# Two tiles of attention output turned by DMA instead of TensorE, in a linear-attention plus GEGLU kernel

## The chip, the cores and the metric

The kernel runs on one core of one Trainium2 chip. The metric is the device time of one execution in microseconds (us); lower is better. A core has five engines with an instruction queue each, which work in order and wait for one another through semaphores: TensorE (PE), VectorE (DVE), ScalarE (ACT), GpSimd (POOL) and SyncE (SP). SP and POOL here mostly issue DMAs, which 16 DMA engines carry out.

## The reference

Eight batches, eight heads, 576 positions, head width 64. The result of the attention is laid out as 4608 tokens by 512 channels and goes through a gated feed-forward layer of width 1536. What is computed, cut to what matters:

```python
def phi(x, c, s):                       # c, s: cos and sin of the position
    r = np.maximum(x, 0.0)
    return np.concatenate([r * c, r * s], axis=-1)      # 64 -> 128 features
q_p, k_p = phi(q, cos_w, sin_w), phi(k, cos_w, sin_w)
kv  = np.einsum('bhsf,bhsd->bhfd', k_p, v)
z   = np.sum(k_p, axis=2)
num = np.einsum('bhsf,bhfd->bhsd', q_p, kv)
den = np.einsum('bhsf,bhf->bhs', q_p, z)[..., None] + 1e-06
x   = (num / den) as 4608 x 512
g   = x @ w_gate
out = (gelu(g) * (x @ w_val)) @ w_out
```

## The kernel before, in words

**Attention, by batch.** `prep` (L151) makes one column group of `phi(q)` or `phi(k)`: the cosine half on DVE (L161) or the sine half on ACT (L159); `js` are the nine column groups of a batch. `kv_unit` multiplies keys and values of a batch. `turn_q` (L190) transposes `phi(q)` of a batch with two DMA transposes on SP's queue, as `turn_j` does on TensorE for the first two batches. `nm_unit` (L279) takes one tile of 128 positions: eight matmuls (L281), then three DVE instructions (`den`, `rec` and the product `x_sb`, L292 to L294). A batch has five such tiles; tile 4 overlaps tile 3 by half.

**Turning a tile.** The feed-forward layer wants x with the channels on the partitions. `turn_x_pe` (L352) does this with four TensorE transposes into PSUM (L356) and an ACT copy for each piece (L360); `turn_x` (L345) does it with one DMA transpose for each piece on SP's queue (L348). A piece is the part of a tile that lies in one block of 512 tokens. Tile 3 of batch 1 has two pieces: 64 tokens at the end of block 1, and 64 at the start of block 2.

**Feed-forward, by block.** Nine blocks `n` of 512 tokens, twelve units `jt` of 128 hidden columns. `gv_unit` (L366) does one unit: four gate matmuls into one PSUM bank, four value matmuls into the next (L375), Gelu on ACT (`gel`, L383), the product with the value bank on DVE (`hT`, L384). It uses two pairs of banks in turn, so unit u+2 needs the banks of unit u again: its gate matmuls wait for the Gelu of unit u, and its value matmuls for the product of unit u. A unit can be done for half of the tokens only (`c0`, `w`), which makes matmuls of 256 columns instead of 512. `o_part` (L402) multiplies by `w_out` for one tile of 128 tokens (L405), copies the result on ACT (L414) into one of four `o_sb` buffers, and puts it on the list `stores`; `flush` (L397) issues what is on the list, two DMAs of 128 KB for each tile.

**The order of the work** is written out by hand: each engine runs its instructions in the order in which the program issues them. Around the change it is as follows. The list `order` (L528) runs the output parts of block 0 between the turns and tiles of batch 1, and ends with the turn of tile 2. Then comes block 1 in the loop at L584. Its first two units are in halves, in the order (unit 0, low), (unit 1, low), (unit 0, high), (unit 1, high), with tile 3 turned behind the first of them. The low half of block 1 is made of tile 4 of batch 0, tile 0 and half of tile 1 of batch 1; the high half of tiles 1, 2 and 3. Between the units stand the last column groups of `phi(q)` of batch 2, then `turn_q(2)`, tile 4 of batch 1, and `phi(k)` of batch 2 in thirds (`prep_third`). The table `q3` says behind which unit each column group of `phi(q)` of batch 3 is made. The q of batch 3 is loaded by SP ahead of block 1 (L556). POOL's queue carries loads, and at the end the two casts of v of batch 2 (L558).

Of the kernel before, what the change touches and what calls it, by code (L numbers as in the profile page):

```python
# [16 lines left out]
def kernel(  # L17
# [13 lines left out]
    nc = tc.nc  # L31
# [8 lines left out]
    R = S // 64  # L40
# [4 lines left out]
    JA = 4  # L45
# [31 lines left out]
    def load(eng, name, b, m0, m1, j0=0, j1=R):  # L77
        if (name, b) not in staged:
            staged[name, b] = inp.tile([128, NP, R * D], FP32, name=name + "f")
        eng.dma_start(  # L80
            out=staged[name, b][:, m0:m1, j0 * D:j1 * D],
            in_=rows(srcs[name], b)[:, m0:m1, j0 * D:j1 * D],
        )
# [67 lines left out]
    def prep(name, b, part, js, m0=0, m1=NP, eng=None):  # L151
        dst = phi_tile(name, b)
        src = staged[name, b]
        tab = (cos_t, sin_t)[part]
        for j in js:
            o = dst[:, m0:m1, j, part * D:(part + 1) * D]
            i = src[:, m0:m1, j * D:(j + 1) * D]
            if eng is nc.scalar:
                nc.scalar.activation(o, i, AF.Relu, scale=tab[:, j:j + 1])  # L159
            else:  # L160
                (eng or nc.vector).tensor_scalar(  # L161
                    o, i, 0.0, tab[:, j:j + 1], op0=ALU.max, op1=ALU.mult
                )
# [13 lines left out]
    def cast_v(b, m0, m1, copy, j0=0, j1=R):  # L177
        copy(  # L178
            vx_tiles[b % 2][:, m0:m1, j0:j1, 0:D],
            staged["v", b][:, m0:m1, j0 * D:j1 * D].rearrange("p m (j d) -> p m j d", d=D),  # L180
        )
# [8 lines left out]
    def turn_q(b):  # L190
        for i in range(2):
            nc.sync.dma_start_transpose(
                out=qt_tile(b)[:, i].rearrange("f m (j p) -> f (m j) p", p=64),
                in_=phi["q", b][64 * i:64 * i + 64].rearrange("p m j f -> p (m j f)"),
            )
# [156 lines left out]
    def turn_x_pe(b, t, to, copy):  # L352
        x = xs.pop((b, t))
        p = bank16(to)[:, 0:CT * 128].rearrange("p (c n) -> p c n", c=CT)
        for ct in range(CT):
            nc.tensor.transpose(  # L356
                out=p[:, ct, :], in_=x[:, ct * 128:(ct + 1) * 128], identity=ident
            )
        for blk, c, o, m in pieces(b, t):
            copy(xT_block(blk)[:, :, c:c + m], p[:, :, o:o + m])  # L360
# [5 lines left out]
    def gv_unit(n, jt, c0=0, w=BLK):  # L366
        xt = xT[n]
        js = slice(jt * 128, (jt + 1) * 128)
        b0 = 2 * (turn[0] % 2)
        turn[0] += 1  # L370
        if n not in hT:
            hT[n] = ffn.tile([128, JT, BLK], BF16, name="hT")
        for g, wt in ((0, wg_sb), (1, wv_sb)):
            for ct in range(CT):
                nc.tensor.matmul(  # L375
                    bank(b0 + g)[:, 0:w],
                    lhsT=wt[:, ct, js],
                    rhs=xt[:, ct, c0:c0 + w],
                    start=(ct == 0),
                    stop=(ct == CT - 1),  # L380
                )
        gel = ffn.tile([128, BLK], FP32, name="gel")
        nc.scalar.activation(gel[:, 0:w], bank(b0)[:, 0:w], AF.Gelu)  # L383
        nc.vector.tensor_mul(  # L384
            hT[n][:, jt, c0:c0 + w], gel[:, 0:w], bank(b0 + 1)[:, 0:w]
        )
# [3 lines left out]
    def store(engs, i, o_sb, c0=0, c1=C):  # L390

        for n, eng in enumerate(engs):
            b, j = divmod(2 * i + n, R)
            dst = out[b * S:(b + 1) * S, c0:c1].rearrange("(p j) c -> j p c", j=R)[j]
            eng.dma_start(out=dst, in_=o_sb[64 * n:64 * n + 64, c0:c1])

    def flush():  # L397
        for i, o_sb in stores:
            store((nc.sync, nc.sync), i, o_sb)
        stores.clear()  # L400

    def o_part(i, jts, to, copy):  # L402
        n, tt = divmod(i, 4)
        for jt in jts:
            nc.tensor.matmul(  # L405
                bank(to),
                lhsT=hT[n][:, jt, tt * 128:(tt + 1) * 128],
                rhs=wo_sb[:, jt, :],
                start=(jt == 0),
                stop=(jt == JT - 1),  # L410
            )
        if JT - 1 in jts:
            o_sb = outp.tile([128, C], FP32, name="o_sb")
            copy(o_sb, bank(to))  # L414
            flush()
            stores.append((i, o_sb))


# [1 line left out]
    HALF = BLK // 2  # L420
# [93 lines left out]
    for jt in range(JH, JT):  # L514
# [16 lines left out]
        + [("q8", 2), ("o", 1, 4), ("o", 2, 4), ("kv",), ("q2", 0, 2), ("o", 3, 4)]  # L531
        + [("nm", 0, 2), ("o", 0, 8), ("nm", 1, 6), ("o", 1, 8), ("xt", 0, 4), ("nm", 2, 2)]
        + [("q2", 2, 3), ("o", 2, 8), ("xt", 1, 5), ("nm", 3, 6), ("q2", 3, 4), ("o", 3, 8)]
        + [("xt", 2, 4)]
    )
    for what, *a in order:
        if what == "o":
# [15 lines left out]
            nm_unit(1, a[0], a[1])  # L553
        if what == "xt":
            turn_x_pe(1, a[0], a[1], act_copy)
    for m in (0, 2):  # L556
        load(nc.sync, "q", 3, m, m + 2)
    for m in (0, 2):  # L558
        cast_v(2, m, m + 2, pool_copy)


    def prep_third(name, b, i):
# [4 lines left out]
    def loads(b, names=("q", "k", "v")):  # L567
# [5 lines left out]


    q3 = {
        (1, 8): ((0,), (0, 1)),
        (1, 9): ((1,), (2, 3)),
        (1, 10): ((2,), (4, 5)),
        (1, 11): ((3, 4, 5), (6, 7)),
        (2, 0): ((6, 7), (8,)),  # L580
        (2, 1): ((8,), ()),
    }
    turn[0] = 1
    for n in range(1, NB):  # L584
        b = n + 1
        t_kv, t_nm, t_q, t_k = {1: (5, 8, 12, 12), 2: (5, 7, 7, 9), 3: (2, 5, 6, 9)}.get(
            n, (1, 2, 4, 8)
        )
        for jt in range(JT):
            if n > 3 or jt > 1:  # L590
                gv_unit(n, jt)
            else:
                for i in range(2):
                    gv_unit(n, i, jt * HALF, HALF)
                    if n == 1:
                        j = JA + 2 * jt + i
                        prep("q", b, 1, (j,), eng=nc.scalar)
                        prep("q", b, 0, (j,))
                        if jt == i == 0:
                            turn_x_pe(1, 3, 5, act_copy)  # L600
            if jt % 3 == 1:
                flush()
            if b < B:
                if n == 1 and jt == 2:
                    prep("q", b, 0, (R - 1,))
                    prep("q", b, 1, (R - 1,), eng=nc.scalar)
                    turn_q(b)
                    nm_unit(1, NT - 1)
                if n == 1 and jt == 3:
                    turn_x(1, NT - 1)  # L610

                late = -(-(BLK - 64 * b) // 128)
                nms = [(b, jt - t_nm)] if 0 <= jt - t_nm < (late if n == 1 else NT) else []
                if n == 2 and jt < 2:
                    nms.append((n, 3 + jt))
                i = jt - t_nm - 1
                if 0 <= i < late:
                    turn_x(b, i)
                    if n == 1 and i == late - 1:
                        loads(b + 1, ("k", "v"))  # L620
                for bt in nms:
                    nm_unit(*bt)
                if jt == t_kv:
                    kv_unit(b)
                i = jt - 2 if n <= 2 else -1
                if 0 <= i < 3:
                    prep_third("k", b, i)
                i = jt - (3 if n == 2 else 0)
                if n in (2, 3) and 0 <= i < 2:
                    cast_v(b, 2 * i, 2 * i + 2, dve_copy)  # L630
                i = jt - 9
                if n > 2 and 0 <= i < 2 and b + 1 < B:
                    cast_v(b + 1, 2 * i, 2 * i + 2, dve_copy)
                if (n, jt) in q3:
                    cosines, sines_ = q3[n, jt]
                    prep("q", 3, 1, sines_, eng=nc.scalar)
                    prep("q", 3, 0, cosines)
                if n > 1 and b + 1 < B:
                    if 0 <= jt - t_q < 3:
                        prep_third("q", b + 1, jt - t_q)  # L640
                    if 0 <= jt - t_k < 3:
                        prep_third("k", b + 1, jt - t_k)
                for c, t in nms:
                    if t == NT - 1:
                        if c + 1 < B:
                            turn_q(c + 1)
                        if c + 2 < B:
                            loads(c + 2)
                        for i in range(-(-(BLK - 64 * c) // 128), NT):
                            turn_x(c, i)  # L650
            if n > 1:
                o_part(
                    4 * (n - 1) + jt // 3,
                    range(4 * (jt % 3), 4 * (jt % 3) + 4),
                    4,
                    act_copy,
                )
# [47 lines left out]
```

## Time and profile before

| | |
|---|---|
| median of 5 runs | 329.09 us (327.19 to 329.83) |
| the profiled execution: its own time, its span | 327.04 us, 324.9 us |
| PE busy | 315.3 us, 97% of the span |
| DVE, ACT, POOL busy | 52%, 49%, 9% |
| mean granted TensorE clock | 0.998 |
| mean DMA rate | 165 GB/s |

The profile is of one execution; its time lies 2.05 us below the median of the runs, and its span 2.1 us below its own time. Times inside the trace count from the start of the span. A matmul's duration in the trace is modelled and overlaps the next one, so the spacing of TensorE work is read from starts.

### The profile page before, as it was taken

The page shows a single profiled execution, that of the slowest core. Times are in us where ns is not written, and L with a number is a line of the kernel's source. Part 1 is how long each engine was busy: PE and PEld are TensorE (multiplying, and loading weights), DVE is VectorE, ACT ScalarE, POOL GpSimd, SP SyncE. Part 2 cuts the span into 40 slices and gives each one's busy share as a digit, 9 for nine tenths or more (in the row PEclk, how much of TensorE's full clock was granted, in tenths as well). Part 3 has the DMA queues.
Part 4 walks back from the last instruction along what each step waited for, and adds up shares of the span by engine and source line. Part 5 has one row for each costly group of instructions (what it writes and reads, how often), then busy time and mean ns, then how long its engine had stood idle before and what let it go on. Part 6 is the DMA issues. An engine that isn't in the chain of part 4 may idle for free.

```text
span 324.9 us, 6295 instructions
## 1 busy us (share of the span) xinstructions
PE 315.3 (97%) x2401; PEld 164.9 (51%) x2438; DVE 167.8 (52%) x406; ACT 159.9 (49%) x341; POOL 28.3 (9%) x43
## 2 busy tenths in 40 slices
PE   8899999999999999999999999999999999999995
PEld 3585556556554564445544545445544444444443
DVE  5863666749665961793585348544532222222211
ACT  8865767947455833674457336642222333222220
POOL 2855462000000000000000000000000000000000
PEclk9999999999999999999999999999999999999999
DMA  7999999992999999989979992764531111111124
GB/s 264 259 190 273 303 347 335 221 137 50 307 135 356 241 99 255 296 161 173 366 154 128 305 292 46 105 105 99 90 70 35 35 32 32 35 32 32 34 66 97
DMA packets 69102, 53.57 MB, mean 165 GB/s; under 512 B 45392, under 2 KB 54352, under 8 KB 69072
## 3 DMA queue, kind: packets, MB, share of 16 engines
q1 hardware_dynamic: 59264, 41.23, 55.0%
q0 software_dynamic: 9648, 11.80, 15.8%
q8 instruction: 19, 0.31, 0.4%
q10 hardware_dynamic: 160, 0.13, 0.1%
q14 instruction: 11, 0.09, 0.1%
HBM read 37.75 MB, written 9.44 MB: 145 GB/s over the span
## 4 chain that ended last, share of the span: by engine, by line
PE 93%; DMA 3%; DVE 1%; issue 1%; SPq 1%; DVEq 0%
PE ps L375 57%; PE ps L405 27%; PE ps L281 3%; DMA qf<-in_q_dram 3%; PE ps L240 3%; PE ps L666 1%; SPq L80 1%; PE ps L203 1%; PE ps L356 1%; DVE qp L161 0%; DVE x_sb L321 0%; DVE hT L384 0%; DVE o_sb L673 0%; DVE rec L317 0%; PE ps L139 0%
## 5 line engine op out<-in xcount | busy, mean ns | idle before, releaser
L384 DVE TENSOR_TENSOR hT<-gel,ps 128x512 bf16<-128x512 f32 (+2 forms) x120 | 75.9, 634 | 131.8 <-PE ps L375 127.5
L383 ACT ACTIVATE gel<-ps 128x512 f32<-128x512 f32 (+2 forms) x120 | 66.7, 556 | 109.8 <-PE ps L375 106.1
L375 PE MATMUL ps<-xT,wg_sb 128*128 128x512 bf16 (+2 forms) x473 | 112.2, 357 | 0.6 <-issue 0.2
L375 PE MATMUL ps<-xT,wv_sb 128*128 128x512 bf16 (+2 forms) x472 | 112.2, 357 | 0.5
L405 PE MATMUL ps<-wo_sb,hT 128*128 128x512 bf16 x400 | 102.5, 379 | 1.6 <-issue 1.0
L375 PEld LDWEIGHTS <-wv_sb 128*128 128x128 bf16 x480 | 46.4, 98 | 47.4 <-DMA wv_sb<-in_moe_w_val_dram 0.4
L375 PEld LDWEIGHTS <-wg_sb 128*128 128x128 bf16 x480 | 45.8, 98 | 45.8
L405 PEld LDWEIGHTS <-hT 128*128 128x128 bf16 x420 | 38.4, 98 | 39.8
L414 ACT COPY o_sb<-ps 128x512 f32<-128x512 f32 x34 | 19.9, 585 | 29.4 <-PE ps L405 28.3
L159 ACT ACTIVATE qp<-qf,sin_t 128x256 bf16<-128x256 f32 x71 | 31.8, 502 | 1.7 <-DMA qf<-in_q_dram 1.7
L159 ACT ACTIVATE kp<-kf,sin_t 128x256 bf16<-128x256 f32 (+1 forms) x75 | 30.4, 477 | 0.9 <-DMA kf<-in_k_dram 0.9
L294 DVE TENSOR_TENSOR x_sb<-ps,rec 128x512 bf16<-128x512 f32 x38 | 26.3, 691 | 1.5 <-DVE rec L293 0.2
L161 DVE TENSOR_SCALAR qp<-qf,cos_t 128x256 bf16<-128x256 f32 x71 | 21.7, 353 | 4.3 <-DMA qf<-in_q_dram 4.3
L281 PEld LDWEIGHTS <-qT 128*128 128x128 bf16 x304 | 14.6, 98 | 7.7 <-issue 0.2
L161 DVE TENSOR_SCALAR kp<-kf,cos_t 128x256 bf16<-128x256 f32 x63 | 18.2, 348 | 0.0
L281 PE MATMUL ps<-kv_sb,qT 128*128 128x65 bf16 x304 | 16.0, 194 | 0.0
L249 ACT CAST kv_sb<-ps 128x260 bf16<-128x260 f32 x14 | 4.6, 382 | 13.1 <-PE ps L240 13.1
L139 PE MATMUL ps<-dummy 128*128 128x512 bf16 x28 | 9.0, 477 | 1.5 <-POOL dummy L113 1.5
L240 PEld LDWEIGHTS <-kp 64*128 64x128 bf16 x504 | 8.6, 94 | 3.1 <-issue 3.0
L178 DVE CAST vx<-vf 128x1152 bf16<-128x1152 f32 x12 | 9.2, 769 | 0.8 <-DMA vf<-in_v_dram 0.8
L240 PE MATMUL ps<-vx,kp 64*128 64x65 bf16 x504 | 9.5, 191 | 0.0
L293 DVE RECIPROCAL rec<-den 128x8 f32<-128x8 f32 x38 | 7.7, 203 | 1.3
(52 smaller groups left out, 91.6 us busy)
## 6 DMA issues: line engine op xcount, KB each, us to landing
out_dram<-o_sb SPq DMA_DIRECT2D x70, 128.0 KB, 2.5
kf<-in_k_dram SPq DMA_DIRECT2D x12, 576.0 KB, 6.6
vf<-in_v_dram SPq DMA_DIRECT2D x12, 576.0 KB, 8.8
qf<-in_q_dram SPq DMA_DIRECT2D x10, 576.0 KB, 5.4
qf<-in_q_dram POOLq DMA_DIRECT2D x4, 576.0 KB, 12.1
kf<-in_k_dram POOLq DMA_DIRECT2D x4, 576.0 KB, 12.8
vf<-in_v_dram POOLq DMA_DIRECT2D x4, 576.0 KB, 10.8
wg_sb<-in_moe_w_gate_dram POOLq DMA_DIRECT2D x6, 256.0 KB, 9.0
```

Of the source, the lines that this page charges most:

```text
L139: nc.tensor.matmul(bank(to), lhsT=dummy[:, 0:128], rhs=dummy, start=True, stop=True)
L159: nc.scalar.activation(o, i, AF.Relu, scale=tab[:, j:j + 1])
L161: (eng or nc.vector).tensor_scalar(o, i, 0.0, tab[:, j:j + 1], op0=ALU.max, op1=ALU.mult)
L178: copy(vx_tiles[b % 2][:, m0:m1, j0:j1, 0:D], staged["v", b][:, m0:m1, j0 * D:j1 * D].rearrange("p m (j d) -> p m j d", d=D),)
L240: nc.tensor.matmul(bank(6 + i)[:, m * (D + 1):(m + 1) * (D + 1)], lhsT=kp[rr, m, j, :], rhs=vx[rr, m, j, :], start=(j == 0), stop=(j == R ...
L281: nc.tensor.matmul(bank(b0 + h // 4)[:, (h % 4) * (D + 1):(h % 4 + 1) * (D + 1)], lhsT=q_cols(b, t, h), rhs=kv_sb[b][:, h // 2, h % 2, :], ...
L294: nc.vector.tensor_tensor(x, nm[:, :, :, 0:D], rec[:, :, :, None].to_broadcast([128, 2, 4, D]), op=ALU.mult,)
L375: nc.tensor.matmul(bank(b0 + g)[:, 0:w], lhsT=wt[:, ct, js], rhs=xt[:, ct, c0:c0 + w], start=(ct == 0), stop=(ct == CT - 1),)
L383: nc.scalar.activation(gel[:, 0:w], bank(b0)[:, 0:w], AF.Gelu)
L384: nc.vector.tensor_mul(hT[n][:, jt, c0:c0 + w], gel[:, 0:w], bank(b0 + 1)[:, 0:w])
L405: nc.tensor.matmul(bank(to), lhsT=hT[n][:, jt, tt * 128:(tt + 1) * 128], rhs=wo_sb[:, jt, :], start=(jt == 0), stop=(jt == JT - 1),)
L414: copy(o_sb, bank(to))
```

## The change

- Tiles 2 and 3 of batch 1 are turned by DMA on SP's queue (three DMA transposes) instead of on TensorE.
- In block 1 the first four units are in halves instead of the first two: four low halves, then four high halves. Column groups 4, 5, 6 and (7, 8) of `phi(q)` of batch 2 stand behind the four low halves.
- `turn_q(2)` comes behind unit step 1 instead of step 2.
- The load of q of batch 3 comes behind `turn_q(2)` on SP's queue, and its column groups start one unit later.
- The eight stores of block 0 are no longer issued by SP as the tiles come; GpSimd issues them all, behind its casts of v of batch 2.

```diff
-    def flush():
+    def flush(eng=nc.sync):
         for i, o_sb in stores:
-            store((nc.sync, nc.sync), i, o_sb)
+            store((eng, eng), i, o_sb)
         stores.clear()
...
             copy(o_sb, bank(to))
-            flush()
+            if n > 0:
+                flush()
             stores.append((i, o_sb))
...
-        + [("xt", 2, 4)]
     )
...
-    for m in (0, 2):
-        load(nc.sync, "q", 3, m, m + 2)
+    for t in (2, 3):
+        turn_x(1, t)
     for m in (0, 2):
         cast_v(2, m, m + 2, pool_copy)
+    flush(nc.gpsimd)
...
     q3 = {
-        (1, 8): ((0,), (0, 1)),
-        (1, 9): ((1,), (2, 3)),
-        (1, 10): ((2,), (4, 5)),
-        (1, 11): ((3, 4, 5), (6, 7)),
-        (2, 0): ((6, 7), (8,)),
-        (2, 1): ((8,), ()),
+        (1, 9): ((0,), (0, 1)),
+        (1, 10): ((1,), (2, 3)),
+        (1, 11): ((2, 3, 4), (4, 5, 6)),
+        (2, 0): ((5, 6), (7,)),
+        (2, 1): ((7, 8), (8,)),
     }
...
-            if n > 3 or jt > 1:
+            heads = (0, 4, 2, 2)[n] if n < 4 else 0
+            if jt >= heads:
                 gv_unit(n, jt)
             else:
                 for i in range(2):
-                    gv_unit(n, i, jt * HALF, HALF)
-                    if n == 1:
-                        j = JA + 2 * jt + i
-                        prep("q", b, 1, (j,), eng=nc.scalar)
-                        prep("q", b, 0, (j,))
-                        if jt == i == 0:
-                            turn_x_pe(1, 3, 5, act_copy)
+                    half, unit = divmod(2 * jt + i, heads)
+                    gv_unit(n, unit, half * HALF, HALF)
+                    if n == 1 and jt < 2:
+                        js = ((4,), (5,), (6,), (7, 8))[2 * jt + i]
+                        prep("q", b, 1, js, eng=nc.scalar)
+                        prep("q", b, 0, js)
...
+                if n == 1 and jt == 1:
+                    turn_q(b)
+                    loads(b + 1, ("q",))
                 if n == 1 and jt == 2:
-                    prep("q", b, 0, (R - 1,))
-                    prep("q", b, 1, (R - 1,), eng=nc.scalar)
-                    turn_q(b)
                     nm_unit(1, NT - 1)
```

## The prediction

> **What bounds the kernel now.** I read the chain that ended last first, then the busy times by stage, then the timeline where the change lies.
>
> ```profile
> PE 93%; DMA 3%; DVE 1%; issue 1%; SPq 1%; DVEq 0%
> ```
> ```profile
> 55.00:63.00 8.00, 7.95 (x66) 5.48 (x65) 5.60 (x15) 7.48 (x21) 2.04 (x2) 1.00 0.90 265
> ```
>
> The first line is the chain: 93% of the span is TensorE itself. The second is the stretch of the change, 55 to 63 us: TensorE is busy 7.95 of 8.00 us, DVE 5.60, ACT 7.48 (fifth and sixth pair of columns). So an edit here gains only what it takes from TensorE's stream, and loses whatever makes that stream wait. The next view is the timeline of that stretch.
>
> ```profile
> 53.53 0.69 DVE L294 TENSOR_TENSOR x_sb<-ps,rec 128x512 bf16<-128x512 f32 x1
> ...
> 54.88 0.69 DVE L294 TENSOR_TENSOR x_sb<-ps,rec 128x512 bf16<-128x512 f32 x1
> ...
> 56.20 0.39 PE L356 MATMUL ps<-ident,x_sb 128*128 128x128 bf16 x4
> ...
> 56.42 0.60 PE L375 MATMUL ps<-xT,wg_sb 128*128 128x256 bf16 x4
> ...
> 57.42 0.60 PE L375 MATMUL ps<-xT,wg_sb 128*128 128x256 bf16 x4
> ...
> 59.17 1.03 PE L375 MATMUL ps<-xT,wg_sb 128*128 128x512 bf16 x4
> ...
> 62.46 0.69 DVE L294 TENSOR_TENSOR x_sb<-ps,rec 128x512 bf16<-128x512 f32 x1
> ...
> 62.88 1.03 PE L375 MATMUL ps<-xT,wg_sb 128*128 128x512 bf16 x4
> 63.07 0.87 DVE L161 TENSOR_SCALAR kp<-kf,cos_t 128x256 bf16<-128x256 f32 x3
> ...
> 63.85 0.68 DVE L384 TENSOR_TENSOR hT<-gel,ps 128x512 bf16<-128x512 f32 x1
> ```
>
> The x of tile 2 is ready at 54.22 (53.53 + 0.69), of tile 3 at 55.57. The four transposes of a tile take 0.22 us of TensorE (56.20 to 56.42), a half unit 0.87 us (two from 57.42 to 59.17), a whole unit 1.73 us. Between 56.42 and 57.42 lies one half unit and 0.13 us of waiting for tile 3's copies. The last three DVE rows, from 62.46 on, belong to a burst in front of a product, which matters below. The last view is that of the line which turns tiles by DMA, over the whole span and from 70 to 83 us.
>
> ```profile
> L348 SPq DMA_TRANSPOSE xT<-x_sb x34: 1171/1242/2872, 70.7 to 236.3; - x34
> ...
> DMA to landing us min/median/max: 2.3/3.3/10.8
> ```
> ```profile
> DMA to landing us min/median/max: 2.4/2.4/2.9
> ```
>
> SP is taken 1.2 us by each issue, and the tile lands 2.3 to 2.5 us after its issue begins when the DMA engines are quiet, later behind other transfers (5.5 at 134.5, 9 to 10.8 behind six loads).
>
> **What the Trainium skill says.** VectorE: DVE Perf Modes, section The three transpose paths, gives 1309 ns for a DMA transpose of 128x128 and 390 ns for TensorE's. Here TensorE's cost 54 ns each in the stream (0.22 / 4), and a DMA issue 1.2 us, with 2.4 to land. DMA: Bandwidth & Descriptors, section Anatomy of one DMA, fits about 2.0 us plus bytes / 436e3; for a tile's 128 KB that is 2.3 us, as the trace has it, and says that latency, not volume, is the price. The same page, section Queues, rings and completion order, has each DMA engine take turns between queues packet by packet: GpSimd's stores will share with SP's transposes, not stand in front of them. No row of the trace shows the two together. TensorE: Matmul & The Clock Gate, section Architectural detail, calls ACT and DVE strictly first in, first out; the burst above agrees: the product at 63.85 could have started by 63.15 (its matmuls end at 62.88, and L384 follows by 0.27) and stood behind three cosines.
>
> **The change, part by part.**
>
> *Transposes off TensorE.* Eight go: 2 x 0.22 = 0.44 us from the path, and with the copies the wait of 0.13 us. Three copies go from ACT (0.62 + 2 x 0.35, 1.3 us), which is off the path.
>
> *Halves.* Two more whole units become four halves: 4 x 0.865 against 2 x 1.73 us, nothing on TensorE. The order after, by starts: low halves at 55.13 (tile 1's copy ends at 55.06), 56.00, 56.86, 57.73; high halves 58.60, 59.46; tile 4's `nm_unit` 60.33; high halves 60.58, 61.45; unit 4 at 62.31, against 62.88 before. **Gain 0.57 us**, if nobody is late.
>
> *The wait added.* The high half at 58.60 waits for the first two DMA transposes. SP is free now, the six stores ahead of it being gone: tile 2 issued 54.27 to 55.5, tile 3's first piece at 55.63, landing at 58.0 with 2.4 us. Slack 0.6 us. Who else is on the DMA engines: from 52 to 54.3 they are 98% busy with v(2) and the stores. From 52 to 56.2 v's queue moves 0.84 MB and SP's 0.42 MB; without SP's part, v needs 0.84 MB / 0.355 MB per us = 2.4 us and is done by about 54.4. GpSimd's casts (2 x 1.15) then end near 55.6, and its stores (0.72 us an issue, by its load rows) meet tile 3's landing. I put that at 0 to 0.6 us, which the slack holds: price 0. From both sides: 0, and 2.5 us if it takes 5.5 us as at 134.5. Behind this wait, TensorE's whole queue is held.
>
> *DVE's burst.* Halved units leave half the time between a product and the reuse of its bank. Behind the low halves DVE ends cosines 7 and 8 at about 59.9, the first two high products by 61.0; then the burst, tile 4's three instructions and three cosines of k(2), takes 1.91 us (before: 62.03 to 63.94). The product of the third high half comes at 62.85 to 63.27; unit 4's value matmuls want its bank at 62.31 + 0.87 = 63.18, and 0.07 for the semaphore. **Loss 0.15 us**; bounds 0 and 1.0, the latter if the sines of k(2) on ACT (1.30 us) also hold up the Gelu of that half, which my count ends 0.1 us before its bank is wanted. Before, the same product had 0.9 us to spare (64.53 against 65.46).
>
> *SP's queue.* It loses eight stores, gains three transposes. `turn_q(2)` goes from 62.26 to about 60.0, when the last sine and cosine of q(2) are done; its second half lands 2.2 us earlier than 73.0, where tile 0 of batch 2 wanted it at 73.07 without waiting. Price 0. The loads of q(3) move from 56.73 to about 68.5, behind that turn, and land after 4.7 and 5.5 us (those behind the next turn, at 96.15): 74.0. First use is on ACT behind unit 9's Gelu, near 74.4 (74.88 less the 0.4 gained). A lateness of 1 to 2 us there delays the next Gelu, not TensorE, two units ahead in banks: price 0; bounds 0 and 0.5. The turn of tile 4 follows the loads on SP, at 69.6 instead of 70.66. Behind three times the bytes the trace has 10.1 us; a third of the excess gives 5 us, so 74.6, wanted by block 2 near 78.6.
>
> *q(3)'s sines and cosines* bunch at units 11 and block 2's start: three sines before block 2's first Gelu instead of two, 0.45 us, while the product there waits for DVE in either case (80.75). `turn_q(3)` comes some 0.3 us later, wanted 3 us after its landing. Price 0.
>
> *Stores on POOL.* Nothing is queued behind them but the end. The four `o_sb` buffers are wanted again at 88.03; eight issues from 55.6 end near 61.4 and land by 65. Price 0.
>
> **Sum:** -0.57 + 0.15 = -0.42 us against the profiled 327.04, so 326.6; from unit 5 on TensorE's order is the same and gapless, so it is carried to the end. The profiled execution lies 2.05 us below the median; with the same offset the median goes from 329.09 to **328.7**. 0.5% is 1.6 us, about what a measurement of this kernel can tell from no change.
>
> **Rivals.**
> 1. *The tiles land late* (slower): TensorE waits at the first high half. For: 2.3 to 2.5 us needs quiet engines, and GpSimd's eight stores, never seen beside a transpose here, start just then. Against: v(2) is done by then, and they share. It decides from a landing of 3.4 us on (0.6 slack plus 0.42 gained); with 5.5 us it costs 2.5, so +2.1: 331.2. Chance 0.20, of which beyond +1.6 us less than half.
> 2. *ACT and DVE become the bound of the halved units*: the burst costs 1.0 instead of 0.15, +0.4: 329.5. For: ACT is 94% busy there. Against: three copies are taken from it. Chance 0.13.
> 3. *q(3) or tile 4 late*: the latter lands after 10.1 us, 79.7 against 78.6, a wait of 1.1 us: +0.7, 329.8. Against: two loads stand ahead, not six. Chance 0.05.
> My forecast has 0.62.
>
> **Numbers.** The forecast's own range, 328.3 to 329.2, widens by the spread of a median (five runs span 2.6 us) and by the rivals: 327.6 to 330.6. Faster by over 0.5% needs 1.6 us, more than the whole 0.57 us on offer, so only by scatter: 0.06. Slower comes from rival 1's tail and scatter: 0.13. Same: 0.81.
>
> **What would show it.** Right: no L356 rows after 54 us; a gapless TensorE from 55.1; unit 4 starting near 62.4; tile 3 landing by 58.5. Wrong: a TensorE wait on DMA at the first high half, on DVE or ACT at unit 4, or at block 2's start.

## The result, and the profile after

| | before | after |
|---|---|---|
| median of all runs | 327.87 us (326.47 to 330.02, 79 runs) | 329.28 us (327.45 to 331.05, 44 runs) |
| ratio after / before | | 1.0034, interval 1.0021 to 1.0048 |
| profiled execution: its own time, its span | 327.04 us, 324.9 us | 327.99 us, 326.2 us |

The forecast was 0.12% faster (-0.42 us), in effect no change. The kernel is 0.34% slower, with an interval that excludes 1. The ratio is that of the means; the medians alone would give 1.0043, because the runs of before fall into two groups some 2 us apart, and its median lies between them (the first five runs had 329.09 us). The experiments come to that. Of all runs below, one (of the first experiment) was slow by its clock and is left out of the ratios.

The page of after, the chain that ended last by engine:

```profile
PE 88%; DMA 6%; DVE 2%; issue 1%; ACT 1%; SPq 1%; DVEq 0%; ACTq 0%
```

DMA has gone from 3% to 6% of it, PE from 93% to 88%. The busy times in the stretch of the change (PE, PEld, DVE, ACT and POOL, each with its instructions, then clock, DMA share and GB/s):

```profile
55.00:63.00 8.00, 7.95 (x76) 6.89 (x76) 7.35 (x20) 7.36 (x21) 6.38 (x10) 1.00 0.64 151
```

TensorE is as full as before, 7.95 us of 8.00: nothing is lost in the stretch itself. POOL has gone from 2.04 to 6.38, which is the stores. The timeline of after there:

```profile
54.36 3.89 SPq L348 DMA_TRANSPOSE xT<-x_sb  x3
...
55.22 0.60 PE L375 MATMUL ps<-xT,wg_sb 128*128 128x256 bf16 x4
...
57.52 4.21 POOL L395 DMA_DIRECT2D out_dram<-o_sb  x8
...
58.71 0.60 PE L375 MATMUL ps<-xT,wg_sb 128*128 128x256 bf16 x4
...
60.46 0.42 PE L281 MATMUL ps<-kv_sb,qT 128*128 128x65 bf16 x8
...
60.95 4.88 SPq L192 DMA_TRANSPOSE qT<-qp  x1
...
62.46 1.03 PE L375 MATMUL ps<-xT,wg_sb 128*128 128x512 bf16 x3
...
63.36 0.81 PE L375 MATMUL ps<-xT,wv_sb 128*128 128x512 bf16 x3
```

Each row here is a group of like instructions with its start and duration. The low halves begin at 55.22, the first high half at 58.71 without a wait, tile 4's `nm_unit` at 60.46, unit 4 at 62.46 instead of 62.88. Since this execution runs 0.12 us later than the one of before already at the transposes of q(1) (40.00 against 39.88), the gain at unit 4 is 0.54 us. The three turns of tiles 2 and 3, in the same stretch:

```profile
DMA to landing us min/median/max: 2.4/2.5/3.1
```

So the tiles land in time. Ten microseconds later comes the loss, in TensorE's waits from 50 to 90 us (total us, how often, longest):

```profile
PE ps L281 <- DMA qT<-qp: 1.3, 1, 1.3
```

and, in the chain of that stretch (start, duration, what):

```profile
65.88 8.05 DMA qT<-qp
73.94 0.05 issue
73.98 0.40 PE ps L281 x7
```

Tile 0 of batch 2 is reached at 72.50 instead of 73.07. Its first head runs, and the other seven wait for the second half of `turn_q(2)`, which lands at 73.94. In before there was no such wait, but hardly any cover: the half landed at 73.00, tile 0 began at 73.07, and its second head, the first that needs that half, at 73.10. The two halves of that turn in before (duration on SP's queue in ns, starts, landing times):

```profile
L192 SPq DMA_TRANSPOSE qT<-qp x2: 3688/4129/4570, 62.3 to 66.9; - x2
...
DMA to landing us min/median/max: 6.1/6.3/6.5
```

and in after:

```profile
L192 SPq DMA_TRANSPOSE qT<-qp x2: 4109/4496/4884, 61.0 to 65.9; - x2
...
DMA to landing us min/median/max: 7.6/7.8/8.1
```

The turn is issued only 1.3 us earlier (61.0, not 60.0). The first half takes 7.6 us to land instead of 6.5, the second 8.1 instead of 6.1. What shares the DMA engines just then, from 57 to 62 us (queue: packets, MB, share of 16 engines), in before:

```profile
q1 hardware_dynamic: 648, 1.35, 94.3%
```

and in after, with the issues of the stores:

```profile
q0 software_dynamic: 242, 0.68, 56.4%
q1 hardware_dynamic: 566, 0.13, 12.8%
...
out_dram<-o_sb POOLq DMA_DIRECT2D x8, 128.0 KB, 4.1
```

In before SP's queue q1 moved q(3) and the last stores there, and all but three of their packets were through when the turn's began, at 63.5. In after the stores are on GpSimd's queue q0, and their packets go on until 67.7, beside the turn's.

Offsets of after against before, less the 0.12 us: -0.54 us at unit 4, -0.69 at tile 0 of batch 2, +0.77 behind the wait, +0.78 at block 2's first low half, +0.95 at its first high half, +1.18 at the end.

### The profile page after: what moved, and what is told of

It reads as the page before. It is cut to its first block, busy times and chain, and to the rows that moved or that the text cites. A ratio compares the mean times of both kernels' runs of the same rounds, so it can differ in the third digit from the quotient of the medians.

```text
span 326.2 us, 6326 instructions
## 1 busy us (share of the span) xinstructions
PE 314.4 (96%) x2409; PEld 165.7 (51%) x2446; DVE 168.7 (52%) x408; ACT 159.2 (49%) x340; POOL 32.4 (10%) x51
## 4 chain that ended last, share of the span: by engine, by line
PE 88%; DMA 6%; DVE 2%; issue 1%; ACT 1%; SPq 1%; DVEq 0%; ACTq 0%
PE ps L375 53%; PE ps L405 27%; DMA qf<-in_q_dram 3%; PE ps L281 3%; DMA qT<-qp 2%; PE ps L240 2%; PE ps L666 1%; DMA out_dram<-o_sb 1%; SPq L80 1%; PE ps L203 1%; PE ps L356 1%; DVE qp L161 0%; DVE x_sb L321 0%; ACT kp L159 0%; ACT qp L159 0%
## 5 line engine op out<-in xcount | busy, mean ns | idle before, releaser
L375 PEld LDWEIGHTS <-wv_sb 128*128 128x128 bf16 x488 | 47.2, 98 | 46.6 <-issue 0.3
L375 PEld LDWEIGHTS <-wg_sb 128*128 128x128 bf16 x488 | 46.6, 98 | 45.5 <-DMA xT<-x_sb 0.3
L161 DVE TENSOR_SCALAR qp<-qf,cos_t 128x256 bf16<-128x256 f32 x71 | 22.2, 363 | 4.8 <-DMA qf<-in_q_dram 4.8
L161 DVE TENSOR_SCALAR kp<-kf,cos_t 128x256 bf16<-128x256 f32 x63 | 18.1, 347 | 0.0
L139 PE MATMUL ps<-dummy 128*128 128x512 bf16 x28 | 8.3, 448 | 1.5 <-POOL dummy L113 1.5
L178 DVE CAST vx<-vf 128x1152 bf16<-128x1152 f32 x12 | 9.2, 768 | 0.8 <-DMA vf<-in_v_dram 0.8
```

Source lines behind the costliest of these rows:

```text
L139: nc.tensor.matmul(bank(to), lhsT=dummy[:, 0:128], rhs=dummy, start=True, stop=True)
L161: (eng or nc.vector).tensor_scalar(o, i, 0.0, tab[:, j:j + 1], op0=ALU.max, op1=ALU.mult)
L178: copy(vx_tiles[b % 2][:, m0:m1, j0:j1, 0:D], staged["v", b][:, m0:m1, j0 * D:j1 * D].rearrange("p m (j d) -> p m j d", d=D),)
L375: nc.tensor.matmul(bank(b0 + g)[:, 0:w], lhsT=wt[:, ct, js], rhs=xt[:, ct, c0:c0 + w], start=(ct == 0), stop=(ct == CT - 1),)
```

## The experiments

Two theories stood after the first profile, for why the turn of q(2) lands late: the **stores**, which GpSimd now issues beside it, or the **loads of q(3)**, which now stand behind it. A third was the turn's own start, bound by the single qT buffer.

### Moving the two parts

**q(3) loaded ahead of block 1 again**, all else as after:

```diff
     for t in (2, 3):
         turn_x(1, t)
+    loads(3, ("q",))
...
                     turn_q(b)
-                    loads(b + 1, ("q",))
```

> The changed kernel with one edit undone: SP loads q(3) ahead of block 1 again, directly behind the turn of tile 3, and not behind the turn of q(2). Theory A (the q(3) loads behind the turn of q(2) delay the completion of its second half): the second half lands by 72.5 us instead of 73.9, TensorE's wait before tile 0 of batch 2 falls from 1.46 us to under 0.3, and the kernel is about 1.2 us faster than the changed one: 0.3 us under before, ratio 0.999. Theory B (GpSimd's stores beside the first half are the cause): the loads now fall together with the stores, so nothing is gained: ratio to before 1.003 or more. Theory C (the turn starts too late, as it waits for qT, a single buffer, to be read): as B, 1.003.

330.29 us, ratio 1.0077 (1.0048 to 1.0106). The turn in this kernel, and what waited for it:

```profile
L192 SPq DMA_TRANSPOSE qT<-qp x2: 3442/5456/7469, 60.6 to 68.1; - x2
...
  PEld L281: 2.8, 1
  PE ps L281: 2.5, 1
...
DMA to landing us min/median/max: 6.7/8.1/9.4
```

The wait grows from 1.3 to 2.5 us: with loads and stores both ahead, SP spends 7.5 us on issuing the first half. Beside these stores, then, q(3) ahead of the turn is worse than q(3) behind it.

**Stores issued later**, behind unit 8 of block 1 (`gate` is a spare buffer for a copy that GpSimd must wait for):

```diff
-    flush(nc.gpsimd)
...
+            if n == 1 and jt == 8:
+                nc.gpsimd.tensor_copy(gate, hT[1][:, 8, 0:1])
+                flush(nc.gpsimd)
```

> The changed kernel with one edit altered: GpSimd issues the stores of block 0 behind a copy that waits for hT of unit 8 of block 1 (near 72 us), so nothing but the q(3) loads shares the DMA engines with the turn of q(2). Theory A (q(3) loads): the second half still lands near 73.5 (its issue may begin 0.3 us earlier), the wait stays over 1 us, ratio to before 1.003. Theory B (stores): the turn lands after 6.5 and 6.1 us, at about 71.7, no wait, ratio 0.999.

328.63 us, ratio 1.0033 (1.0014 to 1.0051). TensorE's waits from 50 to 90 us:

```profile
PE ps L375 <- DMA xT<-x_sb: 2.5, 2, 1.6
```

and the turn:

```profile
L192 SPq DMA_TRANSPOSE qT<-qp x2: 3518/3907/4296, 60.8 to 64.4; - x2
...
DMA to landing us min/median/max: 6.1/6.4/6.8
```

The turn lands in 6.1 and 6.8 us, at 71.2, and nobody waits at tile 0, although the q(3) loads still stand behind it. But the stores now meet the turns of batch 2's tiles (three of them with a median of 5.0 us to land, from 73 to 80 us), and TensorE waits at block 2 instead. The loss has only moved.

**Both moves together:** 

> Both edits of the last two: q(3) loaded ahead of block 1, and the stores of block 0 on GpSimd only behind unit 8. Theory A: like the first of them, wait zero, ratio to before 0.998 to 0.999 (the 0.57 us of TensorE's path gained, less 0.04). Theory B: also no wait, same. Theory C (qT's single buffer): the turn begins at 60.95 as in the changed kernel and lands 6.1 to 6.5 us after each issue, near 71.8: wait zero, so C is refuted as a cause by itself if the wait is gone.

328.5 us, 1.0036 (1.0016 to 1.0056). The q(3) packets now run until 65 ahead of the turn, its second half lands at about 75.3, and a wait of 1.1 us stays at tile 0, where none was expected. No store is beside the turn here.

**Before, with q(3) loaded behind the turn**, and with after's table `q3`: 

> The kernel before with one part of the change alone: q(3) is loaded behind the turn of q(2), and its sines and cosines come one unit later; turns on TensorE, halves and stores as before. Theory A: the second half's completion moves from 73.0 to about 75 us, and TensorE, which wants it at 73.07, waits 1.5 to 2 us: ratio to before 1.005 to 1.006. Theories B and C: no stores on GpSimd and no earlier turn here, so the landing stays at 73.0 or comes earlier, as q(3) no longer stands beside the first half: ratio 0.999 to 1.001.

328.85 us, 1.0047 (1.0023 to 1.0071). The profiled execution, at 331.11 us, lies well above that. The turn lands in 6.6 and 7.4 us, with 0.5 us of waiting for it. The larger loss is at block 2's start, in the two waits

```profile
PE ps L375 <- ACT gel L383: 0.9, 1, 0.9
PE ps L375 <- DVE hT L384: 0.7, 1, 0.7
```

where ACT's sines of q(3), for whose load it idles 3.74 us, stand ahead of a Gelu and so of a product. So in before too q(3) costs something when it comes late, by another way than at tile 0.

**Stores as the tiles come**, on GpSimd, ahead of its casts of v(2), then the same with q(3) early:

```diff
             stores.append((i, o_sb))
+            if n == 0:
+                flush(nc.gpsimd)
...
-    flush(nc.gpsimd)
```

> The changed kernel with one edit: GpSimd issues the stores of block 0 as the tiles come (from 52 us), ahead of its casts of v(2), which nobody wants before 66 us. The DMA engines are then free of stores by about 58.5, before the turn of q(2) at 60.9. Theory D (it is the sum of transfers around the turn: a turn of q occupies all DMA engines for about 8.4 us, and stores beside it push it on): the turn lands near 71.2 as with the later stores, no wait at tile 0 of batch 2 (wanted at 72.5), nothing at block 2's start but at most 0.3 us, ratio to before 0.998 to 0.9995, the first version faster than before. Theory A (q(3)'s loads behind the turn are enough by themselves): the wait stays above 1 us, ratio 1.003.

> The last kernel, and q(3) loaded ahead of block 1, directly behind the turn of tile 3. Theory D: its 1.15 MB (3.3 us of the DMA engines) stand ahead of the turn of q(2), which waits for them in the same queue: the second half lands at 73 to 74, TensorE waits about 1 us, ratio to before 1.001 to 1.003. Theory A: no loads behind the turn, no wait, ratio 0.9985.

329.67 us, 1.0052 (1.0032 to 1.0071), and 329.7 us, 1.0045 (1.0026 to 1.0063). Now the tiles' turns are hit: TensorE waits 1.0 and 1.4 us at the first high half, 0 and 0.6 us at tile 0. So this is no better place for them.

**Block 0's stores left out** (`stores.clear()` in place of the flush; 512 rows of the output stay unwritten), and **qT in two buffers** (`attn2.tile` in place of `attn.tile`):

> The changed kernel without the stores of block 0: 512 rows of the output are left unwritten, all else as in the changed kernel. It prices the stores where they stand now. Theory B or D: the turn of q(2) lands after 6.1 and 6.8 us at about 71.2, no wait at tile 0 of batch 2, under 0.3 at block 2: ratio to before 0.998 to 0.9995. Theory A: wait above 1 us, 1.003.

> The changed kernel with two buffers for qT instead of one: the turn of q(2) need not wait until tile 4 of batch 1 has read q(1). Theory C: the turn begins at 60.0 instead of 60.95 and lands about as much earlier, so the wait falls from 1.46 to about 0.6 us: ratio to before 1.001. Theory D: the DMA engines are busy with stores until 62 anyway, its packets begin no earlier, and the wait stays above 1.2: 1.003.

328.42 us, 1.0003 (0.9982 to 1.0024), and 329.12 us, 1.0014 (0.9989 to 1.0038). Neither interval excludes no change, so neither settles its question. In the second the turn was issued at 61.65, ahead of tile 4's `nm_unit` at 63.58, which shows that the single buffer had bound its start. But TensorE's waits from 50 to 90 us were of another kind there:

```profile
PE ps L375 <- DMA xT<-x_sb: 1.4, 1, 1.4
```

No wait for qT, but one at the first high half, where after had none. The kernel without stores, too, had a small wait there (0.2 us) and none at tile 0. That led to the second part.

### Two kinds of execution

The traces fall into two kinds at about 42 us, long before the change. DVE's nine cosines of k(1) (L161) and GpSimd's casts of v(1) (L178), in the timeline of before:

```profile
42.14 2.45 DVE L161 TENSOR_SCALAR kp<-kf,cos_t 128x256 bf16<-128x256 f32 x9
...
43.30 3.91 POOL L178 CAST vx<-vf 128x1152 bf16<-128x1152 f32 x2 [2.96 <-DMA vf<-in_v_dram]
```

and in that of the kernel with two qT buffers:

```profile
42.01 4.28 DVE L161 TENSOR_SCALAR kp<-kf,cos_t 128x256 bf16<-128x256 f32 x9
...
42.63 1.25 POOL L178 CAST vx<-vf 128x1152 bf16<-128x1152 f32 x1 [2.97 <-DMA vf<-in_v_dram]
```

In the first the cosines run through in 2.45 us and the casts are stretched to 3.91; in the second each cast takes 1.2 us and the cosines are stretched to 4.28. TensorE then waits 1.7 us at 46 us for a copy that is queued on DVE behind them. The cast begins when v(1) has landed, 0.98 to 1.5 us behind the first cosine in the traces of the first kind and 0.6 to 1.15 us in those of the second; the ranges overlap, so that start alone does not decide. In this late kind TensorE is 1.7 us later while SP's and GpSimd's DMAs are not, and what follows collides in other places. The profiled executions of before, of after, of the first three runs above and of the one with both as-they-come stores and early q(3) are of the early kind; the other four above are of the late kind.

I tried to force one kind: the casts of v(1) are held behind a copy of GpSimd that reads `phi(k)` of batch 1, its first column first, then its last:

```diff
-    for m in (0, 2):
-        cast_v(1, m, m + 2, pool_copy)
...
+            nc.gpsimd.tensor_copy(gate, phi["k", 1][:, 0, 0, 0:1])
+            for m in (0, 2):
+                cast_v(1, m, m + 2, pool_copy)
```

> The kernel before with one edit outside the change: GpSimd's casts of v(1) (and the loads of v(2) behind them) wait for the first cosine of k(1). In the profiles so far DVE's nine cosines of k(1), near 42 us, take 2.45 us when they are under way before GpSimd's cast and 4.3 us when the cast starts first, and TensorE then waits 1.7 us at 46: the two populations of the times, about 327 and 329. With DVE always first: single runs all near 327, ratio to before 0.996 to 0.997.

> The changed kernel with the same edit. All runs are then of the kind of the profile of after (TensorE waits 1.5 us at tile 0 of batch 2, gains 0.57, loses 0.2 at block 2's start), so 1.1 us behind the last kernel: near 328.0, ratio to before 1.0 to 1.001. If instead the change loses mainly in the other kind of execution (tiles 2 and 3 late at the first high half), this one lies closer to the last kernel than 0.5 us.

328.63 us (1.003, 1.0012 to 1.0048) for before and 329.06 us (1.0037, 1.0016 to 1.0058) for after. A miss: in both traces the casts behind the first cosine slow the other eight, 4.22 us, and the execution is of the late kind. It is useful as such: by the ratios the change costs 0.07% there (1.0037 / 1.003), by the medians 0.43 us; with intervals of some 0.2% on either side, neither can be told from nothing, nor from the 0.34%. TensorE loses 0.28 us at the first high half and 0.51 us at block 2, and nothing at tile 0.

Each unchanged kernel was profiled once more, to have pairs of one kind:

> The changed kernel, as it is, looked at again. If the cosines of k(1) take 4.3 us in this execution: the phase of TensorE is 1.7 us later, GpSimd's stores start before the turn of tile 3 is issued, and TensorE waits about 1.5 us for xT at the first high half, nothing at tile 0 of batch 2; span near 327.7. If they take 2.45 us: as in the profile of after, span near 326.2.

> The kernel before, as it is, looked at again. If the cosines of k(1) take 4.3 us: TensorE is 1.7 us later from 46 us on and stays so, no wait on a DMA, span near 327. If 2.45: as in the profile of before, span near 324.9.

Both fell in the early kind: after 328.9 us, with 1.6 us of waiting for qT, before 326.61 us, with no DMA wait.

Then the gate on the last sine of k(1) (`phi["k", 1][:, 0, R - 1, D:D + 1]`), in before and in after:

> The kernel before with GpSimd's casts of v(1) held until the last sine of k(1) on DVE (near 45 us), so that DVE's nine cosines of k(1) never run beside a cast. If the two populations of the times come from that meeting: cosines 2.45 us in the profile, no TensorE wait at 46, single runs all near 327, ratio to before 0.996 to 0.998 (GpSimd's edit of the run before, which let DVE begin first, had 4.2 us and 328.6).

> The changed kernel with the same edit. With the phase fixed as in the profiles of before and after, the change costs what those show: the wait at tile 0 of batch 2 (1.5 us) and block 2's start (0.2), less 0.57: 1.1 to 1.5 us slower than the kernel of the run above (ratio between the two 1.0035 to 1.0045), near ratio 1.000 to before.

327.08 us (0.9977, 0.9958 to 0.9996; all runs from 326.46 to 327.88) and 328.2 us (1.0013, 0.9994 to 1.0032). The cosines are back at 2.44 us:

```profile
41.84 2.44 DVE L161 TENSOR_SCALAR kp<-kf,cos_t 128x256 bf16<-128x256 f32 x9
...
45.06 2.24 POOL L178 CAST vx<-vf 128x1152 bf16<-128x1152 f32 x2
```

With the kind held early, the change costs 0.36% (1.0013 / 0.9977, 1.1 us). The held after still scatters, from 327.15 to 329.82. In its profile TensorE waits 1.7 us for qT and loses 1.3 us more in block 2's low half, where q(3) comes late. The held before is also the fastest kernel of this study that does all of the work, 0.23% below before, by an edit that lies outside the change. The rest is measured against this pair.

### The cause, with the kind held

All of these have the casts held as in the last pair.

**q(3) loaded behind tile 4's turn** instead of ahead of it, then **half of the stores held** to unit 2 of block 2 on top of that:

```diff
                 if n == 1 and jt == 1:
                     turn_q(b)
-                    loads(b + 1, ("q",))
...
                     turn_x(1, NT - 1)
+                    loads(b + 1, ("q",))
```

> The changed kernel with that edit, and the loads of q(3) one step later on SP's queue: behind the turn of tile 4, not directly behind the turn of q(2). Theory A (the last packets and the completion of the turn's second half run among the packets of q(3)'s loads, which begin 4.2 us after it): second half lands about 1.5 us earlier, near 72.4, the wait under 0.4 us, 1.1 us faster than the run above. Theory B (the stores beside the first half alone): the wait stays at 1.2 us or more, no gain. q(3) itself lands 1.3 us later, which ACT feels and TensorE not.

> The last kernel, and of the eight stores of block 0 only four behind the casts of v(2); the other four behind a copy that waits for unit 2 of block 2 (near 87 us). Theory B: the first half of the turn has 0.5 MB less beside it, the whole turn lands by 71.8, no wait, and no collision at block 2's start: 0.4 to 0.6 us faster than the kernel before with the same edit, the first version that gains. Theory A alone: as the last kernel.

329.21 us (1.0054, 1.003 to 1.0078) and 328.45 us (1.0018, 1.0002 to 1.0034). TensorE's wait for qT from 50 to 90 us in the first:

```profile
PE ps L281 <- DMA qT<-qp: 1.8, 1, 1.8
```

and in the second:

```profile
PE ps L281 <- DMA qT<-qp: 1.2, 1, 1.2
```

Without the loads behind it the turn still lands after 8.1 and 8.4 us, and the wait is 1.8 us, against 1.7 in the same kernel with the loads. The loads behind the turn are not the cause of that wait. (Later still, they make the kernel 1.0 us slower by the medians.) With half of the stores away the first half lands in 6.2 us, but the second still takes 7.9, and the wait falls only to 1.2, where none was expected. The four stores left were through by 62.9, and nothing of them ran beside the second half.

**No stores of block 0 at all** (again `stores.clear()`), and **the stores alone** moved to GpSimd in the held before:

> After, with the casts of v(1) held behind k(1)'s cosines, and without block 0's stores (512 rows of the output are left unwritten). It stands against the same kernel with the stores (328.2, ratio 1.0013) and the kernel before with the casts held (327.08, ratio 0.9977). If the stores are what holds up the turn of q(2): the second half lands at 72.3 or earlier, no wait above 0.3 us at tile 0 of batch 2, and the 0.5 us gained at unit 4 is kept: 326.5 (ratio 0.996), 1.7 us below the kernel with stores. If something else does (the later issue, the three turns of tiles 2 and 3, the loads of q(3)): the second half still lands near 74, 1 us or more of waiting stays, and the ratio stays over 1.0000.

> Before, with the casts of v(1) held behind k(1)'s cosines, and with one part of the change alone: block 0's eight stores issued by GpSimd behind its casts of v(2). It stands against the kernel before with the casts held (327.08, ratio 0.9977, a wait of 0.4 us at tile 0). If the stores on GpSimd beside the turn of q(2) are the cause: the turn is issued at the same 62 us, both halves land after 7 us or more instead of 6.2 to 6.5, the wait at tile 0 is 1.2 to 2 us, the ratio 1.000 to 1.003. If the cause is rather that the turn comes earlier, amid other transfers: the stores are through or nearly so by 62 us, the landing stays below 6.7 us, and the ratio stays at 0.998.

The first: 326.65 us, ratio 0.9966 (0.9952 to 0.998), all 22 runs from 326.11 to 327.72. The turn:

```profile
L192 SPq DMA_TRANSPOSE qT<-qp x2: 3553/3994/4434, 61.0 to 64.6; - x2
...
DMA to landing us min/median/max: 6.3/6.7/7.1
```

and tile 0 of batch 2 in the timeline:

```profile
72.57 0.42 PE L281 MATMUL ps<-kv_sb,qT 128*128 128x65 bf16 x8
```

The same start at 61.0 as in after, but the second half lands at 71.7 and the eight heads of tile 0 run at 72.57 without a wait. The stores are worth 1.5 us (0.9966 against 1.0013), which is the whole loss and the gain upstream with it. That much is shown: without block 0's stores the loss is gone, in all 22 runs.

The second: 330.04 us, 1.0068 (1.0042 to 1.0093), a miss that tells of another thing. Its chain from 40 to 90 us begins:

```profile
36.37 16.45 DMA qf<-in_q_dram
```

With no stores ahead of it on SP, the load of q(3) issued at 41.74 instead of 56.30. It shared the engines with the loads of q(2), k(2) and v(2), q(2) took 16.45 us to land, and TensorE waited 2.0 us, until 54.6, for a tile made late. The turn was issued at 66.1, 1.8 us after the last of the stores, and landed in 6.5 and 7.4 us. So it says nothing on stores beside a turn. It shows that SP's stores in before also timed the load that stood behind them, and that the change could not move the one without the other.

### What the late half waits for

A half of the turn is 0.59 MB in 2304 packets of 256 bytes. Without the stores the trace has 270 to 280 packets in most half microseconds on all 16 engines, some 30 ns each, which fills them for 4.2 us, twice over for the two halves. The Trainium skill, DMA: Bandwidth & Descriptors, section Queues, rings and completion order, has an engine drain a whole packet of one queue before it turns to the next. The prediction read from it that the stores share and do not stand in front. The trace agrees in so far as packets of both queues pass in the same half microseconds; but the turn alone keeps the engines full, so what it shares it loses. Its first packet starts 1.8 us behind the issue in after and 1.2 us without the stores, its last at 71.9 and 71.1.

In after the three half microseconds from 63.5 have 162, 75 and 197 packets of the turn, at 73, 65 and 36 ns, while 8 to 16 KB of stores pass in each. This alone does not convict the stores: in before, with three packets of a store left, the two half microseconds from 64.0 have 252 and 13, at 85 and 280 ns.

The rest of the delay is behind another queue. Of the 32 packets of 4 bytes with which the second half ends, 30 are through by 71.94, and the last two come at 72.86 and 72.87. In between, one packet of 16 KB on q8, the queue that brings instructions, takes 1.2 us, from 71.68 to 72.88. In three windows of after, 71.45 to 71.96, 71.95 to 72.85 and 72.85 to 72.90:

```profile
q8 instruction: 1, 0.02, 14.7%
```
```profile
DMA packets 41, 0.09 MB, mean 105 GB/s; under 512 B 0, under 2 KB 0, under 8 KB 41
```
```profile
DMA packets 9, 0.02 MB, mean 323 GB/s; under 512 B 2, under 2 KB 2, under 8 KB 9
```

The two late packets end with it to within 0.02 us, here and in five more traces: after once more, the held after, its two variants with q(3) behind tile 4, and "both moves together". In these six, and in the kernel with as-they-come stores and early q(3), the second half lands 0.9 to 1.1 us after the end of such a packet; in the other traces it lands 0.5 to 0.7 us after its own last packet. In two of the seven, "both moves together" and the last named, no store is left when the turn's packets begin. So the wait of 1.1 to 1.8 us at tile 0 in the six ends with a fetch of instructions; that the late packets stood behind it on one DMA engine is read from these times, as the traces shown do not name the engine. Without the stores the same fetch runs from 71.01 to 72.02, but the turn's last packet is through at 71.11, and nothing waits for it.

The change itself brought the fetch there. In before it starts at 74.04, a microsecond after the landing, with 1,712 matmuls and weight loads of TensorE recorded by then; in after at 71.68, with 1,699. The halved units put 32 instructions more in front and the DMA turns take 16 away, so TensorE reaches the same count earlier (1,701 to 1,705 in three more traces; that the fetch goes by this count is read from these numbers). No run moved the fetch alone. An estimate from these figures: with 0.6 us behind its 30th packet the half would have landed at 72.5 in after, just as tile 0 was reached. How much of the 1.5 us is the stores' traffic, and how much the fetch that the delay lets in, stays open.

## Why the prediction was wrong, by its steps

- *Transposes and halves, gain 0.57 us*: right. Unit 4 came 0.54 us earlier, and the order by starts agrees within 0.1 us when the whole is shifted by 0.12.
- *The wait added at the first high half, price 0 to 2.5*: 0 in after's profile (landing 2.4 to 3.1 us). In the late kind 0.28 us in the held kernel and up to 1.4 us in the variants, where a turn landed in 5.2 us beside the stores. That is rival 1, though not in after as profiled. The fit of 2.0 us plus bytes that the prediction cites is given by its page for GpSimd's DMAs; for SP's turns the traces decide.
- *DVE's burst, 0.15 us*: 0.04. Unit 4's value matmuls began at 63.36 instead of 63.32, 0.90 us behind its gate matmuls. Rival 2 did not come.
- *SP's queue: the turn "goes from 62.26 to about 60.0 ... its second half lands 2.2 us earlier than 73.0 ... Price 0"*: **the step that failed**, in two parts. The start was counted by its inputs alone; qT is one buffer, and SP had to wait until tile 4's `nm_unit`, at 60.46 to 60.7, had read q(1) from it: 60.95. And the landing was carried over unchanged, 6.1 to 6.5 us, although the step *Stores on POOL* put eight stores, priced 0, right ahead of it. They moved until 67.7, the halves took 7.6 and 8.1 us, and the second landed at 73.94 instead of 70.8. The term measures 1.46 us, from -0.69 to +0.77, and without the stores it is gone. The fetch of instructions, which no step names, has its share in it.
- The earlier start was not the larger part. The held after issued its turn at 60.14 and the wait was longer, 1.7 us.
- *q(3)'s loads, price 0, bounds 0 and 0.5; q(3)'s sines bunching, price 0*: a second step that failed, by little in after's profile. The loads stand behind the late turn and landed at 75.7 and 77.3 instead of 74.0, so ACT's sines began at 77.39 instead of 74.4. "Delays the next Gelu, not TensorE" did not hold: the Gelu delays a product, and block 2's second low half needs its bank. TensorE loses 0.17 us there in after, 0.37 in the held kernel without stores, 1.3 in the held after. From there to the end another 0.23 us was lost, which was not taken apart. (The 4.7 us that the step reads for a first load is the median of two, 3.92 and 5.49.)
- *Rival 3*: tile 4 landed at 77.60, later than the forecast 74.6, and nobody waited, as block 2 began at 79.98. Its other half, q(3) late, came by the way just told.
- **The sum.** Predicted -0.57 + 0.15 = -0.42. Measured in the pair of profiles -0.54 + 0.04 - 0.19 (from unit 4's value matmuls to tile 0, mostly in `kv_unit`, 1.34 us instead of 1.52) + 1.46 + 0.41 = +1.18 us. Without the stores the held kernel is 0.43 us faster than the held before by the medians (326.65 and 327.08 us), the forecast's number, but only in part by its sum: TensorE is 0.67 us earlier at tile 0, the held before loses 0.25 there by its own turn, and 0.38 goes again at block 2's start. That these nearly cancel is luck.
- The late kind was not foreseen at all. Its share of the runs of either kernel is not known, which is why the 0.34% cannot be split further.

## What to carry to other kernels

Before a step on a DMA queue is priced at nothing, look at how full the engines are while the next large transfer on them is under way, and how much cover its landing has: here 0.1 us. A store that nobody waits for is free only where nobody's load or transpose shares its time, and an earlier start needs its destination free, not only its inputs ready. Look at the small queues too: here the end of a 0.59 MB transpose came 0.9 us late, together with one packet of instructions. When runs scatter in two groups, find where the traces part and hold that fixed before comparing anything.

## What the hardware showed that was not expected

- Nine DVE instructions from fp32 to bf16 (128x256 each) take 2.44 us alone and 4.2 to 4.3 us beside GpSimd's casts of 128x1152; or the cosines keep their 2.45 us and the two casts take 3.91 us instead of 2.24. The Trainium skill, SBUF — State Buffer, section SBUF: two separate sides, tells of a port pair that is locked for a whole instruction by GpSimd or by a DVE instruction of certain modes, whichever starts first, while the other blocks. Whether these cosines are of such a mode no run here shows. The traces agree that one of the two is held up and not both: by 1.8 us or by 1.7 us. Which one it is they do not explain.
- A DMA transpose of 1.18 MB in packets of 256 bytes keeps all 16 engines full for 8.4 us, 140 GB/s, against 270 GB/s that before's loads and stores reach between 57 and 62 us.
- A 16 KB packet on the queue of instructions takes 0.9 to 1.4 us near 72 us, and in six traces the end of a DMA transpose came with its end, 0.9 us behind the rest.
- GpSimd takes 0.53 us to issue a 128 KB store (4.21 / 8), less than the 0.72 us of its loads that the prediction used.
